# Four seven-product units in each tile from tile 3, with one written order for up projection, attention and down projection

## The chip, the cores and the metric

The kernel runs on one core of a Trainium2 chip. Its time is the device time of one execution in microseconds (us). Seven runs of the kernel before took 279.84 to 280.44 us, with a median of 280.2. The profile is of one further execution.

## The reference: pooled attention, then a two-layer network

The keys and values of 8 batches with 8 heads are averaged over groups of 8 positions (576 rows become 72). Each query attends to the 72 pooled keys of its head. The result, 4608 tokens of 512 values, goes through a network with 2048 hidden values and the silu function.

```python
k_p = k.reshape(B, H, Sp, pool, D).mean(axis=3)      # B = H = 8, S = 576, D = 64, pool = 8, Sp = 72
v_p = v.reshape(B, H, Sp, pool, D).mean(axis=3)
scores = scale * np.matmul(q, k_p.transpose(0, 1, 3, 2))
attn = np.exp(scores - np.max(scores, axis=-1, keepdims=True))
attn = attn / (np.sum(attn, axis=-1, keepdims=True) + 1e-09)
x = np.matmul(attn, v_p).transpose(0, 2, 1, 3).reshape(4608, 512)
h = x @ w_in                                         # 512 x 2048
out = (h / (1 + np.exp(-h))) @ w_out                 # 2048 x 512
```

## The kernel before

**Tiles.** The 4608 tokens are worked off in nine tiles of 512 tokens, tile 0 to tile 8. A tile has an *up half* (`up`), which computes the hidden values `h_T` (16 groups of 128, with tokens as columns) from the attention output `xT`, and a *down half* (`down_quarters`, in tile 0 `down`), which computes the output from them. The attention of batch t+1 is done in between: its parts are small functions (`q_transpose`, `k_transpose`, `scores`, `denominators`, `numerators`), called as *fillers*. Each filler has a step number. `spread` counts the matmul steps of a half, and when a step is reached it issues the fillers due. So the order on every engine is the order in which Python issues instructions; no scheduler changes it, and an engine that waits holds up everything behind it in its own queue.

**Seven products instead of eight.** Some matrix products are split in two by two quarters and computed with seven products of sums of quarters instead of eight products. In the down half that is the whole product (products 1 to 7, each 16 matmuls of 256 columns). It needs five sums of quarters of `w_out` (`weight_sum`, made once), five sums of hidden quarters in each tile (`hidden_sum`, product numbers 1, 2, 5, 6, 7), and additions of the seven results on VectorE and ScalarE. In the up half a *unit* of four hidden groups is split in this way: seven products of four matmuls of 256 columns take the place of 16 matmuls of 512 columns. `UNITS` names three units: A is groups 4 to 7, B 8 to 11 and C 12 to 15. They need sums of `w_in` quarters (`unit_weight_sum`, once) and five sums of `xT` quarters in each tile (`unit_x_sum`). Groups 0 to 3 are *plain*: four matmuls of 512 columns each, followed by a silu. Tile 0 is wholly plain; tile 1 uses units A and B only, and the later tiles all three.

**How a unit goes.** `stage(y, n)` issues product n of unit y and what follows it. Product 2 goes to PSUM bank P and ScalarE copies it to `r_sb`; product 5 goes to bank Q and VectorE adds it to `r_sb`, giving `rr_sb`; product 1 goes to bank R and VectorE subtracts, giving `t_sb`. Products 4 and 3 add onto P and Q, and a silu on ScalarE takes each straight from the bank. Products 7 and 6 add onto P and Q again, and VectorE adds `t_sb`, giving `c_sb[0]` and `c_sb[1]`, from which the stages "h" and "s" make the last two silus. Products 7 and 6 have to wait until the silus of 4 and 3 have read their banks. Each of `r_sb`, `rr_sb`, `t_sb` and the two `c_sb` exists once and is passed from unit to unit. Eight PSUM banks are shared: five in turn for P, Q and the attention (`at`), and three in turn for R, plain groups and the down half (`mm`).

**The down half before.** Order of products: 2, 5, 1, 4, 3, 7, 6. Product 2 is copied to `r_sb` and product 5 is added, giving `rr_sb`; product 1 less `rr_sb` gives `t_sb`. Product 4 onto 2 and product 3 onto 5 are two output quarters (a copy on ScalarE and one on VectorE); 7 and 6 onto these, with `t_sb` added, are the other two. The last tile does products 1, 4, 3, 7, 6 for its first 128 tokens of each half and then for the rest, so that stores can start earlier.

**Other queues.** GpSimd pools keys and values (`pool_k`, `pool_v`) and issues nearly all loads. `behind_x_sums` copies one element of an x sum on GpSimd, so that the pooling starts only when that sum is there. SyncE issues the stores.

Of the kernel before, what the change touches and what calls it, by code (L numbers as in the profile page):

```python
# [27 lines left out]
FP32 = mybir.dt.float32  # L28
# [8 lines left out]
def kernel(  # L37
# [53 lines left out]
    def ps_tile(shape, dtype, tag, name):  # L91
        return psum.tile(shape, dtype, tag=tag, bufs=banks[tag], name=name)
# [24 lines left out]
            singles.tile([128, 5, 2, 256], BF16, name=f"w_sum1{n}") for n in range(2)  # L117
        )
    ]
    x_sum = singles.tile([128, 5, 2, NQ], BF16, name="x_sum")  # L120
    gate = singles.tile([128, 1], BF16, name="gate")
    c_sb = [singles.tile([128, 2, NQ], FP32, name=f"c_sb{n}") for n in range(2)]
# [69 lines left out]
        )  # L192
        nc.gpsimd.tensor_add(out=dst, in0=raw[:, :, :D], in1=raw[:, :, D : 2 * D])

    def behind_x_sums():
        nc.gpsimd.tensor_copy(out=gate[:1], in_=x_sum[:1, U_XI[6], 0, :1])

    def pool_k(b):
        pool_rows(kp[:SP], batches[b]["k_raw"])
# [119 lines left out]
    def third(n):  # L319
        return tuple((g, n * QV, (n + 1) * QV) for g in range(2))  # L320
# [78 lines left out]
    def attn_tables():  # L399
        nc.scalar.preload_act_table_set("natural_log_exp_and_others")  # L400
# [13 lines left out]

    UNITS = ((4, 6), (8, 10), (12, 14))
    UW = [
        {
            (i, j): w_in_sb[:, 2 * j : 2 * j + 2, 128 * u : 128 * (u + 2)]  # L420
# [39 lines left out]
    def up(t, fillers, items):  # L460
# [3 lines left out]
                KF if len(it) == 3 else 2 * len(it[1].strip("hs")) for it in items  # L464
            ),
        )
        ps = {}

        def product(y, n, bank, first):
# [45 lines left out]
            else:  # L515
                hidden(y, 1, 1, c_sb[1])

        for it in items:
            if len(it) == 3:
                plain(t, step, *it)  # L520
            else:
                for n in it[1]:
                    stage(it[0], n)
        for _ in step:
            pass

    def plain(t, step, g, n0, n):
        tag = "at" if (t, g, n0) == (0, 3, 0) else "mm"
# [157 lines left out]
            pass  # L686


    warm_ps = ps_tile([128, 512], FP32, "mm", "warm_ps")

    def warm_up(n):
# [97 lines left out]
        " C6 Ch Cs g2 g3",  # L789
    )  # L790
    visits = [third(n) for n in range(3)]
    for t in range(NT):
        a = t + 1
        f_up, f_down = [], []
        if t == 0:
            GA = 11
# [7 lines left out]
        else:  # L804
            G = lambda *gs: [(g, 0, NTT) for g in gs]
            if t == 1:
                items = (
                    G(12, 13, 14, 15) + [(0, "25143"), (1, "2"), (0, "7"), (1, "5")]
                    + [(0, "6h"), (1, "1"), (0, "s")] + G(0) + [(1, "43")] + G(1)
                    + [(1, "7h6")] + G(2) + [(1, "s")] + G(3)  # L810
                )
            else:
                items = []
                for it in THREE[t // B].split():
                    items += [(("BCA".index(it[0])), it[1])] if it[0] in "ABC" else G(int(it[1]))
# [6 lines left out]
            f_up.append((56, lambda: hidden_sum(6, 4, 8)))  # L822
            for n, k0 in ((2, 0), (5, 0), (1, 4), (1, 0)):
                f_up.append((64, lambda n=n, k0=k0: hidden_sum(n, k0, k0 + 4)))
            f_down.append((33, lambda: hidden_sum(7, 0, 8)))
            f_down.append((71 if t < B else 50, lambda: hidden_sum(6, 0, 4)))

        for n, t0, f_to, at, parts in (
            (1, 0, f_down, 48, (0, PW)), (3, 0, f_down, 52, (0, PW)),
            (6, 0, f_down, 8, (0, PW)), (4, 0, f_down, 12, (0, 2)),  # L830
            (7, 0, f_down, 14, (0, 2)), (4, 1, f_down, 20, (2, PW)), (7, 1, f_down, 52, (2, PW)),
        ):
            for i in range(*parts):
                if t == t0:
                    f_to.append((at + i, lambda n=n, i=i: weight_sum(n, i)))
# [63 lines left out]
        if t == 1:  # L899
            def unit_weight_tiles():  # L900
                k_w = big.tile([128, 4, 2, 256], BF16, tag="k_raw2", name="w_sum12")
                v_w = big.tile([128, 4, 2, 256], BF16, tag="v_raw2", name="w_sum12")
                w_sum1.append([k_w[:, i] for i in range(4)] + [v_w[:, 0]])

            f_down.append((72, unit_weight_tiles))
            for i, n in enumerate(U_W):
                f_down.append((73 if i < 2 else 81, lambda n=n: unit_weight_sum(2, n)))
        if t != 1:
            moe_tables()
        if t == 0:  # L910
# [34 lines left out]
```

## Time and profile before

| | |
|---|---|
| profiled execution | 279.88 us, of which 278.1 us are the span from the first to the last instruction |
| median of seven runs | 280.2 us |
| busy: TensorE, VectorE, ScalarE, GpSimd | 271.7, 220.7, 189.2, 98.3 us |
| a tile with attention (tile 3's down half and tile 4's up half) | 28.77 us |
| silus of plain groups / of units from a bank / from `c_sb` | 592 / 603 and 598 / 628 ns each |
| VectorE addition out of PSUM, 128x512 | 681 to 692 ns each |
| hidden sum, 128x1024 | 684 ns each |
| table load on ScalarE | 1283 ns each |

Busy times are summed over the instructions of an engine. The recorded end of a matmul is modelled, and matmuls are pipelined, so how fast they go is read from the distance of their starts. The order in time shows merged groups: start, length to the last end, engine, line, operation, what it writes and reads, the shape and the count; square brackets give idle time ahead of the group and what ended it. PEld are the weight loads of TensorE.

### The profile page before, as it was taken

The numbers are of one execution on the slowest core, as the hardware profiler recorded it, in microseconds if no ns is written. First come the engines' busy times: TensorE is split into PE (matmuls) and PEld (weight loads), VectorE is DVE, ScalarE is ACT, GpSimd is POOL, SyncE is SP. The second block draws the span as 40 slices with busy tenths as digits, with TensorE's granted clock in tenths as the row PEclk, the third lists the DMA queues.
The fourth block names the chain that finished last, engine by engine and source line by source line (L and its number), as shares of the span: only waits on it lengthen the run. The fifth ranks groups of instructions, "written<-read, shape, count | busy, mean of one in ns | idle before, by whom it ended". The sixth has DMA issues, their size and how long they took to land.

```text
span 278.1 us, 7140 instructions
## 1 busy us (share of the span) xinstructions
PE 271.7 (98%) x2857; PEld 203.2 (73%) x2877; DVE 220.7 (79%) x415; ACT 189.2 (68%) x369; POOL 98.3 (35%) x104
## 2 busy tenths in 40 slices
PE   8999999999999999999999999999999999999995
PEld 4448444576778677867888788687877778788784
DVE  4986777898998976897689768986888588966982
ACT  1688767468577966797679757985789478326810
POOL 8745217142158430953086207970640000000001
PEclk9999999999999999999999999999999999999999
DMA  7999999885849789569756935599510041005004
GB/s 212 279 250 249 205 320 189 236 173 109 160 61 234 202 119 168 134 175 125 148 117 171 132 61 133 143 128 140 133 50 2 2 104 50 0 11 139 7 0 152
DMA packets 31313, 37.71 MB, mean 136 GB/s; under 512 B 10352, under 2 KB 22256, under 8 KB 31280
## 3 DMA queue, kind: packets, MB, share of 16 engines
q0 software_dynamic: 23920, 27.03, 52.0%
q1 hardware_dynamic: 6928, 9.58, 12.5%
q10 hardware_dynamic: 432, 0.66, 0.7%
q8 instruction: 22, 0.36, 0.5%
q14 instruction: 11, 0.09, 0.1%
HBM read 36.70 MB, written 9.44 MB: 166 GB/s over the span
## 4 chain that ended last, share of the span: by engine, by line
PE 79%; DMA 14%; DVE 3%; issue 1%; ACT 1%; POOL 0%; POOLq 0%; DVEq 0%
PE o_psQ L645 16%; PE o_psP L645 16%; PE u_psP L477 11%; PE u_psQ L477 10%; PE hp_ps L537 10%; DMA w_in_sb<-in_moe_w_in_dram 6%; DMA w_out_sb<-in_moe_w_out_dram 6%; PE o_psR L645 5%; PE u_psR L477 3%; PE sc_ps L340 3%; PE nu_ps L384 2%; DMA q_bf<-in_q_dram 2%; PE den_ps L358 2%; DVE w_sum L623 1%; DVE xT L393 1%
## 5 line engine op out<-in xcount | busy, mean ns | idle before, releaser
L645 PEld LDWEIGHTS <-h_sum 128*128 128x128 bf16 x640 | 60.7, 98 | 11.5 <-DVE h_sum L605 1.3
L477 PEld LDWEIGHTS <-w_sum 128*128 128x128 bf16 x460 | 45.0, 98 | 8.4 <-issue 0.5
L605 DVE TENSOR_TENSOR h_sum<-h_T 128x1024 bf16<-128x1024 bf16 (+1 forms) x72 | 49.7, 743 | 1.0 <-ACT h_T L543 1.0
L537 PE MATMUL hp_ps<-xT,w_in_sb 128*128 128x512 bf16 (+3 forms) x253 | 47.8, 329 | 0.8
L348 ACT ACTIVATE es<-sc_ps 72x384 bf16<-72x384 f32 (+1 forms) x100 | 39.0, 469 | 8.5 <-PE sc_ps L340 8.3
L543 ACT ACTIVATE h_T<-hp_ps 128x512 bf16<-128x512 f32 (+2 forms) x63 | 31.7, 520 | 9.9 <-PE hp_ps L537 7.9
L537 PEld LDWEIGHTS <-w_in_sb 128*128 128x128 bf16 x268 | 25.6, 98 | 15.3 <-issue 1.1
L485 ACT ACTIVATE h_T<-c_sb 128x512 bf16<-128x512 f32 x46 | 28.8, 628 | 4.4 <-DVE c_sb L509 3.1
L393 DVE TENSOR_TENSOR xT<-nu_ps,rec 128x384 bf16<-128x384 f32 (+1 forms) x50 | 24.0, 533 | 4.4 <-PE nu_ps L384 4.3
L645 PEld LDWEIGHTS <-h_T 128*128 128x128 bf16 x256 | 24.1, 98 | 4.5 <-issue 0.9
L549 POOL DMA_DIRECT2D out_dram<-o_sb x2 | 1.2, 617 | 67.9 <-issue 67.2
L367 ACT ACTIVATE lnd<-den_ps 128x384 f32<-128x384 f32 (+1 forms) x23 | 11.1, 483 | 19.8 <-PE den_ps L358 19.8
L190 POOL TENSOR_TENSOR raw<-raw 72x1024 f32<-72x1024 f32 x10 | 23.6, 2362 | 0.1
L500 DVE TENSOR_TENSOR t_sb<-u_psR,rr_sb 128x512 f32<-128x512 f32 x23 | 15.9, 692 | 6.7 <-PE u_psR L477 5.0
L494 ACT COPY r_sb<-u_psP 128x512 f32<-128x512 f32 x23 | 13.4, 585 | 10.7 <-PE u_psP L477 8.0
L477 PEld LDWEIGHTS <-w_in_sb 128*128 128x128 bf16 x184 | 17.6, 98 | 2.4
L497 DVE TENSOR_TENSOR rr_sb<-u_psQ,r_sb 128x512 f32<-128x512 f32 x23 | 15.7, 681 | 3.5 <-ACT r_sb L494 1.6
L645 PE MATMUL o_psP<-w_out_sb,h_sum 128*128 128x256 bf16 x128 | 17.6, 273 | 0.0
L512 DVE TENSOR_TENSOR c_sb<-u_psQ,t_sb 128x512 f32<-128x512 f32 x23 | 15.8, 687 | 2.3 <-PE u_psQ L477 2.1
L509 DVE TENSOR_TENSOR c_sb<-u_psP,t_sb 128x512 f32<-128x512 f32 x23 | 15.8, 686 | 2.2 <-PE u_psP L477 0.9
L645 PE MATMUL o_psQ<-w_sum,h_sum 128*128 128x256 bf16 x128 | 16.7, 273 | 0.0
L645 PE MATMUL o_psQ<-w_out_sb,h_sum 128*128 128x256 bf16 x128 | 16.6, 273 | 0.0
(83 smaller groups left out, 508.2 us busy)
## 6 DMA issues: line engine op xcount, KB each, us to landing
out_dram<-o_sb SPq DMA_DIRECT2D x128, 64.0 KB, 1.8
raw<-in_k_dram POOLq DMA_DIRECT2D x10, 576.0 KB, 8.0
raw<-in_v_dram POOLq DMA_DIRECT2D x10, 576.0 KB, 8.0
q_bf<-in_q_dram POOLq DMA_DIRECT2D x6, 576.0 KB, 10.8
w_in_sb<-in_moe_w_in_dram POOLq DMA_DIRECT2D x8, 256.0 KB, 8.5
w_out_sb<-in_moe_w_out_dram POOLq DMA_DIRECT2D x4, 512.0 KB, 13.3
raw<-in_v_dram POOLq DMA_DIRECT2D x2, 768.0 KB, 11.0
raw<-in_k_dram POOLq DMA_DIRECT2D x1, 768.0 KB, 10.4
```

Source lines behind the costliest of these rows:

```text
L190: nc.gpsimd.tensor_add(out=raw[:, :, : 2 * D], in0=raw[:, :, : 2 * D], in1=raw[:, :, 2 * D :])
L348: nc.scalar.activation(es[:, s, :], sc[s], func=AF.Exp, scale=score_scale)
L393: nc.vector.tensor_mul(out=xT[:, 2 * g0 + c : 2 * (g0 + ng - 1) + c + 1 : 2, cols], in0=nu[c][:, :w].rearrange("r (g n) -> r g n", g=ng), ...
L477: nc.tensor.matmul(ps[y, bank][:, u, :], lhsT=w[:, kk, 128 * u : 128 * (u + 1)], rhs=x[:, kk, :], start=first and u == 0 and kk == 0, stop ...
L485: nc.scalar.activation(h_T[:, g : g + 2, j * NQ : (j + 1) * NQ], src, func=AF.Silu)
L500: tt(out=t_sb, in0=ps[y, "R"], in1=rr_sb, op=ALU.subtract)
L509: tt(out=c_sb[0], in0=ps[y, "P"], in1=t_sb, op=ALU.add)
L512: tt(out=c_sb[1], in0=ps[y, "Q"], in1=t_sb, op=ALU.add)
L537: nc.tensor.matmul(hp_ps[:, r0:r1], lhsT=w_in_sb[:, kk, g * 128 : (g + 1) * 128], rhs=xT[:, kk, x0 : x0 + r1 - r0], start=(kk == 0), stop= ...
L543: nc.scalar.activation(h_T[:, g, n0 : n0 + n], hp_ps[:, :n], func=AF.Silu)
L605: nc.vector.tensor_tensor(out=h_sum[n][:, ks, :], in0=quarter(*a, ks), in1=quarter(*b, ks), op=op)
L645: nc.tensor.matmul(ps[b][:, c, :], lhsT=left(n, kt, c), rhs=W_OUT[n][:, kt, :], start=b not in begun, stop=kt == k1 - 1, skip_group_check= ...
```

## The change

From tile 3 on, `up` and `down_quarters` with their fillers are replaced by `run`, which walks through one written order, `PROGRAM`. A token such as `C2` is stage 2 of unit C, and `Ca` and `Cs` are its last two silus; E is a fourth unit, groups 0 to 3, in place of the plain groups. `d40` is the first quarter (four matmuls) of down product 4. `h2h` and `h2l` are the upper and lower half of hidden sum 2. `q`, `k`, `sc`, `de`, `nu` are the parts of attention (`npp` is the last third of the numerators of the batch before), `x4` an x sum, `T1` and `T2` the table loads. Tiles without attention leave these tokens out.

The order of down products becomes 4, 3, 2, 5, 1, 7, 6. Product 4 is copied to `r_sb`, product 3 added to it, and two more VectorE subtractions (`u1`, `u2`) take the two finished output quarters from `rr_sb`; product 1 then adds `rr_sb`. The output quarter of bank Q is copied by ScalarE instead of VectorE. In the last tile products 1, 7, 6 go by columns.

The weight sums of the fourth unit are made in tile 2's down half. In tile 0 the first halves of weight sums 1 and 3 are made at earlier steps. In tile 1 the stage "s" of unit A moves behind stage 4 of unit B, and hidden sum 7 moves from step 33 to 44.

```diff
+    w_e = singles.tile([128, 2, 2, 256], BF16, name="w_sum1e")
...
-    def behind_x_sums():
-        nc.gpsimd.tensor_copy(out=gate[:1], in_=x_sum[:1, U_XI[6], 0, :1])
+    def behind_x_sums(n=6):
+        nc.gpsimd.tensor_copy(out=gate[:1], in_=x_sum[:1, U_XI[n], 0, :1])
...
-    UNITS = ((4, 6), (8, 10), (12, 14))
+    UNITS = ((4, 6), (8, 10), (12, 14), (0, 2))
...
+        stage = unit_stages(t, step)
...
+    def unit_stages(t, step):
         ps = {}
...
+        return stage
...
+    def down_stages(t, last):
+        ps = {}
+        bank = {2: "P", 5: "Q", 1: "R", 4: "P", 3: "Q", 7: "P", 6: "Q"}
+        begun = set()
+        add, sub = ALU.add, ALU.subtract
+        tt = nc.vector.tensor_tensor
+
+        def matmuls(n, k0, k1, cs=(0, 1)):
+            b = bank[n]
+            for kt in range(k0, k1):
+                for c in cs:
+                    nc.tensor.matmul(
+                        ps[b][:, c, :], lhsT=left(n, kt, c), rhs=W_OUT[n][:, kt, :],
+                        start=b not in begun,
+                        stop=kt == k1 - 1, skip_group_check=True,
+                    )
+                    begun.add(b)
+
+        def after(n, cc=(0, 1), tail=False):
+            cs = slice(cc[0], cc[-1] + 1)
+            if n == 4:
+                nc.scalar.copy(r_sb, ps["P"])
+            elif n == 3:
+                tt(out=rr_sb, in0=ps["Q"], in1=r_sb, op=add)
+            elif n == 2:
+                nc.scalar.copy(o_sb[1][:, :, LO], ps["P"])
+                if last:
+                    store(t, 3, LO, (nc.gpsimd,))
+            elif n == 5:
+                nc.scalar.copy(out=o_sb[0][:, :, HI], in_=ps["Q"])
+                if last:
+                    store(t, 1, HI)
+            elif n == 1:
+                tt(out=t_sb[:, cs], in0=ps["R"][:, cs], in1=rr_sb[:, cs], op=add)
+            elif n == 7:
+                tt(out=o_sb[0][:, cs, LO], in0=ps["P"][:, cs], in1=t_sb[:, cs], op=add)
+                for c in cc:
+                    store(t, c, LO if tail else FULL, (nc.scalar if tail else nc.sync,))
+            else:
+                tt(out=o_sb[1][:, cs, HI], in0=ps["Q"][:, cs], in1=t_sb[:, cs], op=add)
+                for c in cc:
+                    if tail:
+                        store(t, 3, HI, both)
+                    else:
+                        store(t, 2 + c, FULL, (nc.gpsimd if last else nc.sync,))
+
+        def part_of(tok):
+            if tok == "o":
+                return after(6)
+            n = int(tok[1])
+            if tok[0] == "u":
+                src = o_sb[1][:, :, LO] if n == 1 else o_sb[0][:, :, HI]
+                nc.vector.tensor_tensor(out=rr_sb, in0=rr_sb, in1=src, op=sub)
+                return
+            if not ps:
+                for b in "PQR":
+                    ps[b] = ps_tile([128, 2, CQ], FP32, "mm", f"o_ps{b}")
+            i = int(tok[2])
+            k0 = 2 * i if n == 4 else 2 * (i ^ 2)
+            matmuls(n, k0, k0 + 2)
+            if i == 3 and n != 6:
+                after(n)
+
+        def columns(c):
+            for n in (1, 7, 6):
+                matmuls(n, 0, KQ, (c,))
+                after(n, (c,), c == 1)
+
+        return part_of, columns
+
+    PROGRAM = (
+        "C2 C5 B2 q0 C1 C4 B5 C3 A2 q1 B4 C7 Ca C6 B1 B3 A5 B7 Cs E2 B6 A1 Ba A3 E5 Bs "
+        "A4 q2 E4 k q3 A6 E3 A7 Aa As E1 h7h E7 E6 d40 npp Ea d41 Es h2h d42 d43 h5h T1 "
+        "h2l d30 d31 d32 d33 sc0 h1l d20 d21 h6l d22 h5l d23 sc1 de0 h1h d50 d51 d52 "
+        "h6h d53 d10 d11 h7l u1 sc2 de1 d12 u2 d13 d70 nu0 d71 de2 nu1 T2 d72 d73 d60 "
+        "x4 x3 d61 x6 d62 x1 d63 o x7 "
+    )
+
+    def run(t):
+        a = t + 1
+        attn, last = a < B, t == NT - 1
+        stage = unit_stages(t, iter(int, 1))
+        part_of, columns = down_stages(t, last)
+        toks = PROGRAM.split()
+        gate_on = int([x for x in toks if x[0] == "x"][-1][1])
+        attn_toks = ("T1 T2 k npp q0 q1 q2 q3 sc0 sc1 sc2 de0 de1 de2 nu0 nu1").split()
+        if last:
+            i = toks.index("d10")
+            sums = [x for x in toks[i:] if x[0] in "hu"]
+            toks = toks[:i] + sums + ["L0", "L1"]
+        toks = [x for x in toks if attn or x not in attn_toks]
+        if a == B - 1:
+            toks.insert(1 + max(toks.index("de2"), toks.index("nu1"), toks.index("o")), "nu2")
+        if t == T4:
+            toks.insert(0, "T2")
+        if attn:
+            if a + 1 < B - 1:
+                load_q(a + 1)
+            behind_x_sums(6 if t == T4 else gate_on)
+            pool_k(a)
+            if a + 1 < B:
+                load_one(a + 1, "k")
+            pool_v(a)
+            if a + 1 < B:
+                load_one(a + 1, "v")
+                if a + 1 == B - 1:
+                    load_q(a + 1)
+                load_rest(a + 1, "k")
+                load_rest(a + 1, "v")
+        for x in toks:
+            if x[0] in "ABCE" and x[1] in "2514376as":
+                stage("ABCE".index(x[0]), {"a": "h"}.get(x[1], x[1]))
+            elif x[0] == "L":
...
+            elif x[:2] == "nu":
+                numerators(a, visits[int(x[2])])
+            elif not last:
+                unit_x_sum(t + 1, int(x[1]))
...
+    T4 = 3
     for t in range(NT):
         a = t + 1
+        if t >= T4:
+            run(t)
+            continue
...
             if t == 1:
                 items = (
                     G(12, 13, 14, 15) + [(0, "25143"), (1, "2"), (0, "7"), (1, "5")]
-                    + [(0, "6h"), (1, "1"), (0, "s")] + G(0) + [(1, "43")] + G(1)
+                    + [(0, "6h"), (1, "1")] + G(0) + [(1, "4"), (0, "s"), (1, "3")] + G(1)
                     + [(1, "7h6")] + G(2) + [(1, "s")] + G(3)
                 )
...
-            f_down.append((33, lambda: hidden_sum(7, 0, 8)))
+            f_down.append((33 if t > 1 else 44, lambda: hidden_sum(7, 0, 8)))
             f_down.append((71 if t < B else 50, lambda: hidden_sum(6, 0, 4)))
...
         for n, t0, f_to, at, parts in (
-            (1, 0, f_down, 48, (0, PW)), (3, 0, f_down, 52, (0, PW)),
+            (1, 0, f_down, 16, (0, 2)), (3, 0, f_down, 30, (0, 2)),
+            (1, 0, f_down, 46, (2, PW)), (3, 0, f_down, 50, (2, PW)),
             (6, 0, f_down, 8, (0, PW)), (4, 0, f_down, 12, (0, 2)),
             (7, 0, f_down, 14, (0, 2)), (4, 1, f_down, 20, (2, PW)), (7, 1, f_down, 52, (2, PW)),
         ):
...
                 k_w = big.tile([128, 4, 2, 256], BF16, tag="k_raw2", name="w_sum12")
                 v_w = big.tile([128, 4, 2, 256], BF16, tag="v_raw2", name="w_sum12")
                 w_sum1.append([k_w[:, i] for i in range(4)] + [v_w[:, 0]])
+                w_sum1.append([v_w[:, 1 + i] for i in range(3)] + [w_e[:, i] for i in range(2)])
 
             f_down.append((72, unit_weight_tiles))
             for i, n in enumerate(U_W):
                 f_down.append((73 if i < 2 else 81, lambda n=n: unit_weight_sum(2, n)))
+        if t == 2:
+            for i, n in enumerate(U_W):
+                f_down.append((76 + 2 * i, lambda n=n: unit_weight_sum(3, n)))
         if t != 1:
             moe_tables()
         if t == 0:
```

## The prediction, made before the changed kernel was run

> **What bounds the kernel now.** I read the first part of the page, then the busy time by stage, then the order in time of single engines.
>
> ```profile
> ## 1 busy us (share of the span) xinstructions
> PE 271.7 (98%) x2857; PEld 203.2 (73%) x2877; DVE 220.7 (79%) x415; ACT 189.2 (68%) x369; POOL 98.3 (35%) x104
> ```
>
> ```profile
> core 0: us, PE busy (x) PEld busy (x) DVE busy (x) ACT busy (x) POOL busy (x), PEclk, DMA share, GB/s
> 237.72:249.97 12.25, 12.25 (x113) 10.82 (x112) 9.53 (x17) 3.33 (x5) 0.00 (x0) 1.00 0.00 1
> 249.97:262.60 12.63, 12.53 (x101) 9.79 (x101) 9.35 (x15) 9.32 (x18) 0.00 (x0) 1.00 0.33 84
> 124.65:153.42 28.77, 28.77 (x342) 24.21 (x340) 23.33 (x42) 22.12 (x43) 12.65 (x10) 1.00 0.71 140
> ```
>
> TensorE sets the time. The first stage is the down half of tile 7 without attention, 112 matmuls of 256 columns; the second the up half of tile 8, 84 of 256 and 16 of 512; the third a whole tile with attention. From 252.15 to 259.13 sixteen unit products start, so one (four matmuls) takes 0.436 us, 109 ns a matmul, at full clock. 28.77 less 12.25 and 12.63 leaves 3.89 us for attention. TensorE stands still nowhere in such a tile, so only its own work, or a wait newly made, can move the time.
>
> Attention is dearer than its matmuls, as this part of TensorE's order in time shows (start, length with a modelled end, what):
>
> ```profile
> 186.83 0.82 PE L645 MATMUL o_psP<-w_sum,h_T 128*128 128x256 bf16 x6
> 187.58 0.35 PE L358 MATMUL den_ps<-es,ones 72*32 72x384 bf16 x4
> 187.75 0.83 PE L384 MATMUL nu_ps<-es,vp 72*32 72x192 bf16 x32
> 188.51 0.94 PE L645 MATMUL o_psP<-w_sum,h_T 128*128 128x256 bf16 x7
> ...
> 223.01 0.61 PE L645 MATMUL o_psQ<-w_sum,h_sum 128*128 128x256 bf16 x4
> 223.55 0.52 PE L384 MATMUL nu_ps<-es,vp 72*32 72x192 bf16 x16
> 224.00 1.26 PE L645 MATMUL o_psQ<-w_sum,h_sum 128*128 128x256 bf16 x10
> ```
>
> Six matmuls of 109 ns from 186.83 end at 187.48; the next full-array matmul starts at 188.51: denominators with two numerators cost 1.03 us. Four from 223.01 end at 223.45, the next is at 224.00: one numerator alone costs 0.55. Read likewise: scores alone 0.56 (151.32 to 151.88), denominators with scores 0.85 (126.39 to 127.24), denominators with one numerator 0.70 (222.31 to 223.01), key transpose 0.13. So a second numerator in a block costs 1.03 - 0.70 = 0.33, alone 0.55: entering and leaving full-array work costs about 0.11 each.
>
> VectorE is the next engine; its order in time:
>
> ```profile
> 146.48 0.68 DVE L509 TENSOR_TENSOR c_sb<-u_psP,t_sb 128x512 f32<-128x512 f32 x1
> 147.08 0.68 DVE L512 TENSOR_TENSOR c_sb<-u_psQ,t_sb 128x512 f32<-128x512 f32 x1
> ...
> 261.75 4.29 DVE L605 TENSOR_TENSOR h_sum<-h_T 128x1024 bf16<-128x1024 bf16 x7
> ```
>
> An instruction lasts 0.68 us but the next starts 0.60 later; seven hidden sums take 4.29, (4.29 - 0.68)/6 = 0.60 apiece. VectorE's room is judged with 0.60.
>
> Tile 1 does have a stall, in TensorE's and ScalarE's order:
>
> ```profile
> 60.82 1.03 PE L537 MATMUL hp_ps<-xT,w_in_sb 128*128 128x512 bf16 x4
> 62.06 0.60 PE L477 MATMUL u_psP<-x_sum,w_sum 128*128 128x256 bf16 x4 [0.21 <-ACT h_T L485]
> ```
>
> ```profile
> 60.40 0.63 ACT L485 ACTIVATE h_T<-c_sb 128x512 bf16<-128x512 f32 x1 [0.57 <-DVE c_sb L512]
> 60.94 0.58 ACT L543 ACTIVATE h_T<-hp_ps 128x512 bf16<-128x512 f32 x1
> 61.42 0.59 ACT L485 ACTIVATE h_T<-u_psP 128x512 bf16<-128x512 f32 x1
> ```
>
> Four matmuls of 217 ns end at 61.69, yet the second unit's product 7 starts at 62.06, when the silu that reads its bank (61.42 to 62.01) is done; the first unit's last silu stands ahead.
>
> **What the Trainium skill says.** "Perfetto Trace Analysis", Identifying the Most-Contended Engine: matmul busy share does not tell how near the roofline a kernel is. The trace agrees (matmuls recorded at 273 ns follow each other at 109), so I count spacing. "TensorE: Matmul & The Clock Gate", Back-to-back issue gap: 262 cycles at 256 columns, 518 at 512, or 109 and 216 ns at 2.4 GHz; the trace has 109 and 217. Its Part 3 says a weight load overlaps running matmuls only where the row groups differ; the 0.11 us at each change of tiling fits that, though the trace does not show the cause. "VectorE: DVE Perf Modes", The TRN2 errata: an fp32 add of 512 takes 691 ns; the trace has 692.
>
> **The change, part by part.**
>
> *Tile 0's weight sums.* Four of the eight sums that run 46.36 to 49.04 (0.335 apart) move to where VectorE idles (0.74 us before 38.82, 1.03 before 43.18). The attention products behind them then follow their numerators (ready about 49.3) and end near 50.4, not 50.99; tile 1's first matmuls no longer wait. 50.60 to 54.27 is 3.67 us for 16 matmuls of 217 ns, 3.47: gain 0.20.
>
> *Tile 1's order.* Without the silu ahead, group 0's runs at 60.15 (matmuls end 59.95, plus 0.20), unit 1's product 4's from 60.65 to 61.25: product 7 starts on time, saving 0.37. The moved silu now stands before product 3's, which ends near 62.28; product 6, due 62.12, waits to 62.32, where it was 62.55. Net 0.20. The hidden sum moved from step 33 to 44 lets value copies start near 71.2, not 72.38: the block at 72.79 takes 0.84 where its like takes 0.70, gain 0.14. Sum of tiles 0 and 1: 0.54.
>
> *Fourth unit's weight sums.* Five VectorE sums, 5 x 0.335 = 1.7 us, in tile 2's down half, where before the stores of products 3 and 7 VectorE idles 1.05 and 1.11 us. Nothing, with that cover; without it at most 0.6.
>
> *Four units from tile 3.* Sixteen plain matmuls become seven products: the up half takes 28 x 0.436 = 12.21 instead of 12.63. Gain 0.42 in each of six tiles.
>
> *Attention in the new order* (tiles 3 to 6). The blocks were scores; denominators+scores; denominators+two numerators; scores; denominators+numerator; transpose: 0.56+0.85+1.03+0.56+0.70+0.13 = 3.83. They become numerator; scores; scores+denominators, twice; numerator; denominators+numerator; transpose: 0.55+0.56+0.85+0.85+0.55+0.70+0.13 = 4.19. Loss 0.36 a tile, three changes of tiling. Denominators *after* scores are not in the trace; bounds 0.70 (denominators add as little as before a numerator) and 0.95 (one more change); I take 0.85, the mirrored order. Net per tile 0.42 - 0.36 = 0.06, times four 0.24.
>
> *VectorE and ScalarE.* Per tile VectorE gains four unit operations and two output differences and loses a copy, 5 x 0.60 = 3.0 us, on 23.3 of 28.8. ScalarE exchanges four silus for a copy, four silus and the output copy, about 1.1 on 22.1. Does either come late? Count from a tile's first product. The unit additions lag about 1.4 us at first (last output sum and x sum) but catch up: product 7 of the first unit ends at 4.36, its addition by 5.3, and the first reuse of its bank, product 5 of the third unit, is due at 5.67. Before the output products VectorE has a chain with no gap: product 7 of the third unit ends at 25 x 0.436 = 10.90, its addition starts 0.26 later, then eleven more up to the low hidden sum of product 5: it starts at 11.16 + 11 x 0.602 = 17.78 and ends at 18.47. With attention, transpose and two products of xT (0.94) make that 19.54, and its reader is due at 42 x 0.436 + 0.13 + 0.55 + 0.56 + 0.85 = 20.40: 0.86 spare. The low sum of product 2 ends at 17.13, its reader is due at 17.81. In tiles 7 and 8 no attention delays TensorE: the reader is due at 18.31, but the sum is there at 18.47, and signal and weight load add about 0.17. Loss 0.33, net 0.42 - 0.33 = 0.09 a tile, two tiles 0.18.
>
> *DMA and GpSimd.* Same instructions in the same order; stores wait for one engine more. GpSimd's gate now follows the last x sum, about 1.4 us into the tile instead of 1.2; pooled keys come near 5.3, wanted at 9.6. In the last column tile two outputs are stored earlier; the last chain of sum and store is unchanged. Zero.
>
> Sum: 0.54 + 0.24 + 0.18 = 0.96 gain. The profiled execution took 279.88 (278.1 of span, 1.8 around it), so 278.9; the runs' median, 280.2, is 0.3 above it, so 279.2.
>
> **Rivals.**
> (a) *The switches are hidden or cheaper*: if denominators cost 0.70 behind scores, 0.30 more returns in each of four tiles, and if the late sum costs nothing in tiles 7 and 8, 0.66 more: gain 2.8, 277.4. For it: weights are loaded ahead. Against: two lone numerators (49 and 223 us) cost 0.55 both.
> (b) *The switches take all*: scores+denominators at 0.95 adds 0.2 a tile, 0.8 in all: 280.0. For it: three array layouts meet in one block.
> (c) *VectorE becomes the bound, slower*: the chain reaches the low sum of product 2 late. It decides where the chain runs 0.5 us late (0.68 less signal and load); 1.1 us late costs 0.6 in each of four tiles, and about 0.6 more in each of the last two: 3.6 lost less 0.96 gained, 282.8; with half that loss, 281.0. It needs a spacing of 0.66 instead of 0.60 over the eighteen or so instructions of a chain. For it: VectorE's load reaches 26.3 of 28.7. Against: 0.60 holds beside busy GpSimd (146 us).
>
> **How the numbers follow.** Forecast 0.50 (its own range 278.7 to 279.7), (a) 0.19, (b) 0.15, (c) 0.16. A difference under 0.2%, 0.56 us, is not told from none: faster is (a) and nearly all of the forecast, 0.67; same is (b) and a remainder, 0.17; slower (c), 0.16. The range 277.4 to 280.6 takes in (a), (b) and the forecast, and leaves out (c).
>
> **What would show it.** Tile 4's period near 28.7, with up products gapless; two lone numerators at 0.55; scores+denominators at 0.85; in tiles 7 and 8 one wait of 0.3 of weight loads on the low hidden sum of product 5; product 7 of tile 1's second unit without its wait. Waits of unit products on VectorE's additions, tile after tile, would make it wrong; so would attention blocks 0.1 off.

## The result, and the profile after

The changed kernel takes 281.4 us (median of 12 runs, 281.15 to 281.65), the kernel before 280.15 (31 runs): ratio 1.0042, 95% interval 1.0034 to 1.0050. That is 1.25 us slower where 1.0 us faster was predicted, so 2.2 us have to be found. The profiled execution took 281.4 us, 279.5 of them span.

The page of the changed kernel, busy time of each engine:

```profile
## 1 busy us (share of the span) xinstructions
PE 273.0 (98%) x2923; PEld 208.8 (75%) x2933; DVE 240.2 (86%) x455; ACT 193.8 (69%) x379; POOL 98.5 (35%) x104
```

TensorE is busy for as large a share as before, while VectorE has gone from 220.7 to 240.2 us. Busy time by stage, the same three stages as before the change (a whole tile with attention, the down half of tile 7, the up half of tile 8):

```profile
core 0: us, PE busy (x) PEld busy (x) DVE busy (x) ACT busy (x) POOL busy (x), PEclk, DMA share, GB/s
...
150.92:179.82 28.90, 28.82 (x338) 23.68 (x336) 26.23 (x48) 23.04 (x45) 13.12 (x11) 1.00 0.60 119
...
238.19:250.82 12.63, 12.40 (x114) 10.87 (x112) 11.79 (x21) 3.71 (x7) 0.00 (x0) 1.00 0.00 1
250.82:263.42 12.60, 12.39 (x115) 10.95 (x113) 10.24 (x18) 8.95 (x17) 0.00 (x0) 1.00 0.33 85
```

No stage became faster by what it saves. The attention tile takes 28.90 us instead of 28.77 (predicted 28.71), the up half of tile 8 12.60 instead of 12.63 (predicted 12.21), the down half of tile 7 12.63 instead of 12.25 (predicted 12.58). In all three the busy time of TensorE is now 0.08 to 0.23 us short of the stage, where before only the second stage fell short (by 0.10). What it waits for is seen in its order in time (start, length, engine, line, operation, matrix multiplied into what bank, shape, count; in brackets the idle time and what ended it):

```profile
176.84 0.29 PE L212 MATMUL kT_ps<-shifts,kp 128*128 128x72 bf16 x4
176.97 0.60 PE L489 MATMUL u_psQ<-x_sum,w_sum 128*128 128x256 bf16 x4
177.65 0.60 PE L489 MATMUL u_psQ<-x_sum,w_in_sb 128*128 128x256 bf16 x4
...
235.20 0.60 PE L489 MATMUL u_psQ<-x_sum,w_sum 128*128 128x256 bf16 x4
236.01 0.60 PE L489 MATMUL u_psQ<-x_sum,w_in_sb 128*128 128x256 bf16 x4 [0.21 <-DVE rr_sb L509]
```

Behind the key transpose (tiles 7 and 8 have none) come two products, each into a bank Q: product 6 of unit A (at 176.97 and 235.20), the third unit in the order of time, and product 3 of unit E, the fourth (at 177.65 and 236.01), which adds onto E's own product 5. Gapless, the second would start 0.44 us after the first. It starts 0.68 later in tile 5 and 0.81 later in tile 7 (the same in tile 8, at 261.24). So 0.24 us are lost in each of tiles 3 to 6 and 0.37 in tiles 7 and 8: 4 x 0.24 + 2 x 0.37 = 1.70 us. What it waits for is `rr_sb` of unit E, since VectorE must have read bank Q before product 3 may add onto it. VectorE's order in time shows why that is late:

```profile
174.69 0.68 DVE L521 TENSOR_TENSOR c_sb<-u_psP,t_sb 128x512 f32<-128x512 f32 x1
175.29 0.68 DVE L524 TENSOR_TENSOR c_sb<-u_psQ,t_sb 128x512 f32<-128x512 f32 x1
176.07 0.69 DVE L512 TENSOR_TENSOR t_sb<-u_psR,rr_sb 128x512 f32<-128x512 f32 x1
176.90 0.69 DVE L509 TENSOR_TENSOR rr_sb<-u_psQ,r_sb 128x512 f32<-128x512 f32 x1
```

From the first to the second of these is 0.60 us, but from the second to the third 0.78 and on to the fourth 0.83. The third writes `t_sb`, which the second reads; the fourth writes `rr_sb`, which the third reads. Each starts 0.10 to 0.14 us after the recorded end of the one before, where an instruction that has nothing to wait for starts 0.08 to 0.09 before it. The fourth ends at 177.59, and product 3 goes on at 177.65.

(Line 489 issues every unit product, line 705 every down product from tile 3 on, line 610 every hidden sum. In kernels with added lines the numbers are a few higher.)

The rest of the loss lies in the down halves without attention:

```profile
243.43 1.04 PE L705 MATMUL o_psQ<-w_out_sb,h_sum 128*128 128x256 bf16 x8
244.70 1.05 PE L705 MATMUL o_psQ<-w_out_sb,h_sum 128*128 128x256 bf16 x8 [0.23 <-DVE h_sum L610]
...
269.93 1.05 PE L705 MATMUL o_psQ<-w_out_sb,h_sum 128*128 128x256 bf16 x8 [0.23 <-DVE h_sum L610]
...
272.62 1.04 PE L705 MATMUL o_psQ<-w_sum,h_sum 128*128 128x256 bf16 x8
273.66 1.03 PE L705 MATMUL o_psR<-w_sum,h_sum 128*128 128x256 bf16 x8
```

The second half of product 5 starts 1.27 us after the first instead of 0.87: 0.40 in each of tiles 7 and 8. In tile 8 product 1 of the second column starts at 273.66, 0.17 after its turn (272.62 + 0.87): it shares bank R with the first column, which VectorE must have read.

Tiles 0 and 1 show what the prediction said of product 7 of the second unit, in TensorE's and ScalarE's order:

```profile
61.73 0.60 PE L489 MATMUL u_psP<-x_sum,w_sum 128*128 128x256 bf16 x4
62.33 0.60 PE L489 MATMUL u_psQ<-x_sum,w_sum 128*128 128x256 bf16 x4
```

```profile
60.68 0.59 ACT L497 ACTIVATE h_T<-u_psP 128x512 bf16<-128x512 f32 x1
61.16 0.63 ACT L497 ACTIVATE h_T<-c_sb 128x512 bf16<-128x512 f32 x1
61.68 0.60 ACT L497 ACTIVATE h_T<-u_psQ 128x512 bf16<-128x512 f32 x1
```

Product 7 starts when the matmuls ahead end (60.86 + 4 x 0.217 = 61.73), and product 6, due at 62.17, starts at 62.33, behind the silu that ends at 62.28.

### The profile page after: what moved, and what is told of

Read it like the earlier page. It is cut to its first block, busy times and chain, and to the rows that moved or that the text cites. A ratio compares the mean times of both kernels' runs of the same rounds, so it can differ in the third digit from the quotient of the medians.

```text
span 279.5 us, 7356 instructions
## 1 busy us (share of the span) xinstructions
PE 273.0 (98%) x2923; PEld 208.8 (75%) x2933; DVE 240.2 (86%) x455; ACT 193.8 (69%) x379; POOL 98.5 (35%) x104
## 4 chain that ended last, share of the span: by engine, by line
PE 74%; DMA 14%; DVE 9%; issue 2%; POOL 0%; DVEq 0%; POOLq 0%
PE u_psP L489 12%; PE u_psQ L489 11%; PE o_psQ L705 10%; PE o_psP L705 9%; DMA w_in_sb<-in_moe_w_in_dram 6%; DMA w_out_sb<-in_moe_w_out_dram 6%; PE u_psR L489 5%; PE o_psR L705 4%; PE o_psQ L650 4%; PE o_psP L650 4%; PE hp_ps L542 4%; PE sc_ps L341 3%; PE nu_ps L385 3%; PE o_ps L577 2%; DMA q_bf<-in_q_dram 2%; DVE h_sum L610 2%
## 5 line engine op out<-in xcount | busy, mean ns | idle before, releaser
L489 PEld LDWEIGHTS <-w_sum 128*128 128x128 bf16 x532 | 51.7, 98 | 7.1 <-issue 0.3
L705 PEld LDWEIGHTS <-h_sum 128*128 128x128 bf16 x480 | 45.1, 98 | 9.5 <-issue 2.2
L497 ACT ACTIVATE h_T<-c_sb 128x512 bf16<-128x512 f32 x58 | 35.6, 626 | 13.3 <-DVE c_sb L521 13.1
L542 PE MATMUL hp_ps<-xT,w_in_sb 128*128 128x512 bf16 (+2 forms) x151 | 25.9, 317 | 0.3
L489 PEld LDWEIGHTS <-w_in_sb 128*128 128x128 bf16 x232 | 22.5, 98 | 4.6 <-issue 1.8
L548 ACT ACTIVATE h_T<-hp_ps 128x512 bf16<-128x512 f32 (+2 forms) x39 | 18.1, 477 | 5.8 <-PE hp_ps L542 4.8
L542 PEld LDWEIGHTS <-w_in_sb 128*128 128x128 bf16 x156 | 14.6, 98 | 8.5 <-issue 0.8
L705 PEld LDWEIGHTS <-h_T 128*128 128x128 bf16 x192 | 18.5, 98 | 2.7 <-issue 0.6
L489 PE MATMUL u_psQ<-x_sum,w_in_sb 128*128 128x256 bf16 x116 | 17.5, 272 | 0.7 <-DVE rr_sb L509 0.4
L497 ACT ACTIVATE h_T<-u_psQ 128x512 bf16<-128x512 f32 x29 | 17.1, 590 | 1.0 <-PE u_psQ L489 0.7
L497 ACT ACTIVATE h_T<-u_psP 128x512 bf16<-128x512 f32 x29 | 16.7, 598 | 1.2 <-PE u_psP L489 1.1
```

The source lines that it names most:

```text
L489: nc.tensor.matmul(ps[y, bank][:, u, :], lhsT=w[:, kk, 128 * u : 128 * (u + 1)], rhs=x[:, kk, :], start=first and u == 0 and kk == 0, stop ...
L497: nc.scalar.activation(h_T[:, g : g + 2, j * NQ : (j + 1) * NQ], src, func=AF.Silu)
L542: nc.tensor.matmul(hp_ps[:, r0:r1], lhsT=w_in_sb[:, kk, g * 128 : (g + 1) * 128], rhs=xT[:, kk, x0 : x0 + r1 - r0], start=(kk == 0), stop= ...
L705: nc.tensor.matmul(ps[b][:, c, :], lhsT=left(n, kt, c), rhs=W_OUT[n][:, kt, :], start=b not in begun, stop=kt == k1 - 1, skip_group_check= ...
```

## The experiments

My theory: the loss is the wait of the fourth unit's product 3, and that wait comes from the single `rr_sb` and `t_sb`, which make VectorE's neighbours wait for each other. Rivals: VectorE simply has too much to do, whatever the buffers; the order of the products is at fault; the attention blocks cost more than predicted; the tile 0 and 1 edits lose time. All differences below are of medians, against the kernel before (280.07 to 280.15, run beside each experiment) or against the changed kernel's 281.40, which was not run again beside them.

**Tiles 0 and 1 alone**, on the kernel before:

```diff
-                    + [(0, "6h"), (1, "1"), (0, "s")] + G(0) + [(1, "43")] + G(1)
+                    + [(0, "6h"), (1, "1")] + G(0) + [(1, "4"), (0, "s"), (1, "3")] + G(1)
...
-            f_down.append((33, lambda: hidden_sum(7, 0, 8)))
+            f_down.append((33 if t > 1 else 44, lambda: hidden_sum(7, 0, 8)))
...
-            (1, 0, f_down, 48, (0, PW)), (3, 0, f_down, 52, (0, PW)),
+            (1, 0, f_down, 16, (0, 2)), (3, 0, f_down, 30, (0, 2)),
+            (1, 0, f_down, 46, (2, PW)), (3, 0, f_down, 50, (2, PW)),
```

> The kernel before with the edits of tiles 0 and 1 alone (weight sums sooner, the silu moved, hidden sum 7 later). If these edits work as the trace after suggests (TensorE's start of tile 2's up half 0.17 us earlier although the first matmul of tile 1 came 0.26 later), they are worth 0.43 us: 279.7 us. Rival: what they give is taken back in tile 1's down half, where denominators now wait for a late ScalarE: 280.1 us.

279.68 us, ratio 0.9984 (0.9977 to 0.9991): 0.45 us faster than before. So this part of the change gains what it should within 0.1. Tile 2, where the fourth unit's weight sums are made, takes 28.74 us in the changed kernel and 28.73 here, so the loss is wholly in the new order from tile 3 on: 281.40 - 279.68 = 1.72 us slower than without it, where 0.42 faster was predicted.

**Two buffers**: the changed kernel with a second `rr_sb` and `t_sb` for every other unit. They take the place of small early buffers that are no longer used from tile 3 on, and a buffer of reciprocals goes from four to three.

```diff
         def stage(y, n):
+            odd = t >= T4 and y % 2
+            rr, ts = (rr_2, t_2) if odd else (rr_sb, t_sb)
...
-                tt(out=rr_sb, in0=ps[y, "Q"], in1=r_sb, op=ALU.add)
+                tt(out=rr, in0=ps[y, "Q"], in1=r_sb, op=ALU.add)
...
-                tt(out=t_sb, in0=ps[y, "R"], in1=rr_sb, op=ALU.subtract)
+                tt(out=ts, in0=ps[y, "R"], in1=rr, op=ALU.subtract)
```

> The changed kernel with a second rr_sb and t_sb that every other unit uses, everything else in its order (the buffers lie over tiles that are dead after tile 1, and three buffers of reciprocals in place of four). Theory: single buffers make VectorE wait for its own last instruction (0.78 and 0.83 us from start to start in place of 0.60), so the fourth unit's rr comes late and its product 3 waits 0.24 us in each of four tiles and 0.37 in each of the last two, 1.7 us in all: 279.7 us, and the waits are gone. Rival, VectorE simply has too much work: the wait stays or turns up at a later product, 281.2 us.

279.52 us, 1.88 less than the changed kernel and 0.998 (0.9972 to 0.9988) of the one before. VectorE does the same number of instructions (455), but without the pauses. Its order (three lines from one unit earlier, and unit E's `rr_sb`) and TensorE's:

```profile
172.00 0.68 DVE L531 TENSOR_TENSOR c_sb<-u_psQ,t_sb 128x512 f32<-128x512 f32 x1
172.59 0.68 DVE L519 TENSOR_TENSOR t<-u_psR,rr 128x512 f32<-128x512 f32 x1
173.19 0.68 DVE L516 TENSOR_TENSOR rr_sb<-u_psQ,r_sb 128x512 f32<-128x512 f32 x1
...
175.77 0.69 DVE L516 TENSOR_TENSOR rr<-u_psQ,r_sb 128x512 f32<-128x512 f32 x1
```

```profile
176.50 0.60 PE L494 MATMUL u_psQ<-x_sum,w_sum 128*128 128x256 bf16 x4
176.94 0.60 PE L494 MATMUL u_psQ<-x_sum,w_in_sb 128*128 128x256 bf16 x4
```

The distances are 0.59 and 0.60. Unit E's `rr_sb` ends at 176.46, 0.48 before product 3, which follows product 6 after 0.44. The wait of product 5 in tiles 7 and 8 falls from 0.40 to 0.21 as well. With the same amount of work on VectorE, "too much to do" is out for this wait.

**The second `rr_sb` only**: as above, but both units' `t_sb` stay one buffer.

```diff
-            rr, ts = (rr_2, t_2) if odd else (rr_sb, t_sb)
+            rr, ts = (rr_2, t_sb) if odd else (rr_sb, t_sb)
```

> The changed kernel with a second rr_sb only; t_sb stays single. The distance from t_sb to rr_sb should fall from 0.83 to about 0.60, that from c_sb to t_sb stay at 0.78. The fourth unit's rr_sb then comes 0.2 to 0.25 sooner, which is nearly the whole wait of product 3 in tiles 3 to 6 (0.24) and some two thirds of it in tiles 7 and 8 (0.37): the time falls by 4 x 0.22 + 2 x 0.23 = 1.3, to about 280.1. If the single t_sb is what holds VectorE up, it falls by less than 0.4, to 281.0 or more.

279.99 us, 1.41 less than the changed kernel. VectorE's order:

```profile
174.68 0.68 DVE L531 TENSOR_TENSOR c_sb<-u_psQ,t_sb 128x512 f32<-128x512 f32 x1
175.47 0.69 DVE L519 TENSOR_TENSOR t_sb<-u_psR,rr_sb 128x512 f32<-128x512 f32 x1
176.07 0.68 DVE L516 TENSOR_TENSOR rr<-u_psQ,r_sb 128x512 f32<-128x512 f32 x1
```

The pause ahead of the single `t_sb` stays (0.79), the one ahead of the doubled `rr_sb` is gone (0.60). So each pause belongs to its own buffer. Product 3 follows after 0.44 in each of the six tiles, so all of its 1.70 us of waiting are gone. The expected gain of 1.3 was met in part by luck: it left a third of the wait in tiles 7 and 8 standing. About 0.3 us is lost again at the end, where 4.4 us pass from the start of the last product to the end of the span instead of 4.1. The other kernels with two buffers made from the changed one show 4.3 to 4.4 there; why stays open. What the second `t_sb` adds, 0.47, is mostly the sooner hidden sums of tiles 7 and 8: here product 5 still waits 0.39 in tile 7 (242.22 to 243.48 is 1.26 instead of 0.87).

**Two buffers in the kernel before**, the control:

> The kernel before with a second rr_sb and t_sb from tile 3 on, given to every other unit. VectorE's distances of 0.79 to 0.83 between unit operations are in its trace too, but plain groups lie between the units there and no TensorE wait is seen. If what costs is the wait of the fourth unit's product 3, and not the distances as such, the kernel before gains nothing: 280.15 (279.9 to 280.4). If the distances cost time by themselves (the rival: any relief of VectorE helps), it gains about as the changed kernel did, 1 to 1.9: 278.3 to 279.2.

The edit is that of the two buffers, with its side effects (early buffers overlaid, three buffers of reciprocals). 280.22 us, ratio 1.0006 (0.9997 to 1.0014): nothing, so the side effects are no gain by themselves. Its tile takes 28.77 us as before (first unit product of tile 4 at 138.63, of tile 5 at 167.40), though VectorE's distance from `t_sb` to `rr_sb` fell there from 0.83 to 0.61. A pause costs time only where TensorE is waiting at its end; in the kernel before, where plain groups lie between the units, it was not.

**Product 3 later**: the changed kernel with E's product 3 behind A's product 7.

```diff
-        "A4 q2 E4 k q3 A6 E3 A7 Aa As E1 h7h E7 E6 d40 npp Ea d41 Es h2h d42 d43 h5h T1 "
+        "A4 q2 E4 k q3 A6 A7 E3 Aa As E1 h7h E7 E6 d40 npp Ea d41 Es h2h d42 d43 h5h T1 "
```

> The changed kernel with the fourth unit's product 3 behind the third unit's product 7 instead of ahead of it, 0.44 us later in TensorE's order. Theory (one wait at one place): product 3 finds its bank free, 1.7 us back, 279.7 us. Rival (VectorE's rate is the bound): the wait moves to the next reader of VectorE's results and the time stays at 281.2.

280.52 us, 0.88 less than the changed kernel. The profiled execution took 281.62, 1.1 above this median, but it lost that ahead of tile 1, whose first matmul starts at 51.96 instead of 50.86, so the later tiles can be read. TensorE and ScalarE:

```profile
177.92 0.60 PE L489 MATMUL u_psQ<-x_sum,w_sum 128*128 128x256 bf16 x4
178.54 0.60 PE L489 MATMUL u_psP<-x_sum,w_sum 128*128 128x256 bf16 x4
178.97 0.60 PE L489 MATMUL u_psQ<-x_sum,w_in_sb 128*128 128x256 bf16 x4
```

```profile
177.38 0.62 ACT L497 ACTIVATE h_T<-c_sb 128x512 bf16<-128x512 f32 x1
177.90 1.07 ACT L497 ACTIVATE h_T<-u_psP 128x512 bf16<-128x512 f32 x2
```

Product 3 (third line) now waits for nothing, but product 7 ahead of it starts at 178.54 instead of 178.36. It adds onto bank P, which the first of the two silus at 177.90 reads. That silu stands in a row without a gap on ScalarE, which begins at 175.82 with a copy into `r_sb`, and VectorE, late by its pauses, reads `r_sb` until 175.73 (read from the times; not tested). The wait moved: it is 0.18 in each of tiles 3 to 6 and 0.3 in tiles 7 and 8, 1.3 in all, so only 0.4 of the 1.70 came back here. The other 0.4 is product 5 in tiles 7 and 8, which waits 0.21 instead of 0.40. This order alone doesn't cure it.

**The low hidden sum of product 5 sooner**, in tiles 7 and 8 of the changed kernel:

```diff
+        if not attn:
+            toks.remove("h5l")
+            toks.insert(1 + toks.index("d33"), "h5l")
```

> The changed kernel with the low hidden sum of product 5 ahead of those of 1 and 6 in tiles 7 and 8 only. If the 0.40 us gap in product 5 is this sum's place in VectorE's queue: 0.8 us back, 280.6 us. If VectorE's rate is the bound there, product 1 waits in its place: 281.3 us.

281.06 us: 0.34 of 0.8. In tile 7 the down half falls from 12.63 to 12.36; in tile 8 nothing is gained (11.98 from the first down product to the last group, in both kernels), because another sum is late in its place:

```profile
269.86 1.04 PE L705 MATMUL o_psR<-w_sum,h_sum 128*128 128x256 bf16 x8
271.19 1.05 PE L705 MATMUL o_psP<-w_sum,h_sum 128*128 128x256 bf16 x8 [0.29 <-DVE h_sum L610]
```

**Two buffers, and all hidden sums of tiles 7 and 8 in the order of need:**

```diff
+        if not attn:
+            toks = (
+                " ".join(toks[: toks.index("d33") + 1]).replace(" h1l", "").replace(" h6l", "")
+                + " h5l h1h d20 d21 h1l d22 d23 h7l d50 d51 h6h d52 d53 h6l "
+                + ("u1 u2 L0 L1" if last else
+                   "d10 d11 u1 d12 u2 d13 d70 d71 d72 d73 d60 x4 x3 d61 x6 d62 x1 d63 o x7")
+            ).split()
```

> The kernel with two rr_sb and t_sb, and in tiles 7 and 8 (without attention) the hidden sums of the down half in the order in which TensorE needs them. With two buffers alone the time was 279.5. What that kernel still waits: 0.21 before the second half of product 5 in tiles 7 and 8, 0.1 to 0.2 before product 1 in tile 8. If these are only an order on VectorE, the time falls by 0.4 to 0.7, to 278.9 to 279.1. If VectorE has too much to do in that stretch, the wait moves on to products 1 and 7 and the time stays at 279.3 to 279.6.

279.12 us, ratio 0.9962 (0.9950 to 0.9974), 0.40 less than with two buffers alone. TensorE:

```profile
242.50 1.91 PE L712 MATMUL o_psQ<-w_out_sb,h_sum 128*128 128x256 bf16 x16
244.25 1.91 PE L712 MATMUL o_psR<-w_sum,h_sum 128*128 128x256 bf16 x16
...
270.44 1.04 PE L712 MATMUL o_psQ<-w_sum,h_sum 128*128 128x256 bf16 x8
271.76 1.03 PE L712 MATMUL o_psR<-w_sum,h_sum 128*128 128x256 bf16 x8 [0.27 <-DVE t_sb L734]
```

Product 5 takes its 1.75 us, and tile 7 has no wait left. In tile 8 the wait of product 1's second column for bank R has grown from 0.17 to 0.45 (270.44 + 0.87 = 271.31, start 271.76). What it waits for ends a row on VectorE without a gap:

```profile
269.69 1.48 DVE L753 TENSOR_TENSOR rr_sb<-rr_sb,o_sb 128x512 f32<-128x512 f32 x2
271.28 0.42 DVE L734 TENSOR_TENSOR t_sb<-o_psR,rr_sb 128x256 f32<-128x256 f32 x1
```

These are `u1`, `u2` and the sum behind them. Each reads what the one ahead wrote, and they start about 0.80 apart (an instruction of 0.68 leaves 1.48 - 0.68 = 0.80 for the first two). At 0.60 apart the last would start 0.39 sooner, an estimate from these distances, so most of this wait, too, would be pauses. A second buffer can't remove these, since a value passes from one to the next. That VectorE simply has too much to do is thus not shown in tile 8 either. Another order there was not run.

**What a change of tiling costs.** First on the kernel before: the numerators of the previous batch done by themselves, six steps later, instead of beside others.

```diff
-                    f_down.append((nu_at[n], lambda: numerators(a - 1, visits[2])))
+                    f_down.append((62, lambda: numerators(a - 1, visits[2])))
```

> The kernel before with one edit: the third numerators of the previous batch are done by themselves, at step 62 of the down half instead of 56, where they stood beside other numerators. TensorE then changes once more in each tile from full matmuls to matmuls over parts of the array and back. If the change and the return cost 0.21 us together, as the prediction has it, in each of five tiles, the time rises by about 1.1, from 280.15 to 281.2. If they cost nothing by themselves (the time lies in the blocks, wherever they stand): 280.15.

281.31 us, ratio 1.0036 (1.0024 to 1.0048): 1.16 us slower, 0.23 for each of five tiles. TensorE's order shows the two blocks that were one:

```profile
159.58 0.35 PE L358 MATMUL den_ps<-es,ones 72*32 72x384 bf16 x4
159.76 0.50 PE L384 MATMUL nu_ps<-es,vp 72*32 72x192 bf16 x16
160.19 0.83 PE L645 MATMUL o_psP<-w_sum,h_T 128*128 128x256 bf16 x6
160.95 0.51 PE L384 MATMUL nu_ps<-es,vp 72*32 72x192 bf16 x16
161.40 0.28 PE L645 MATMUL o_psP<-w_sum,h_T 128*128 128x256 bf16 x1
```

Six full matmuls end at 160.85 and the next starts at 161.40: the lone numerators cost 0.55, as the prediction read elsewhere. Nothing else in this kernel is changed, so the price is that of leaving full-array matmuls once more and coming back.

Then on the changed kernel, the opposite: the second denominators and the lone numerators moved beside the first numerators.

```diff
-        "A4 q2 E4 k q3 A6 E3 A7 Aa As E1 h7h E7 E6 d40 npp Ea d41 Es h2h d42 d43 h5h T1 "
+        "A4 q2 E4 k q3 A6 E3 A7 Aa As E1 h7h E7 E6 d40 Ea d41 Es h2h d42 d43 h5h T1 "
...
-        "h6h d53 d10 d11 h7l u1 sc2 de1 d12 u2 d13 d70 nu0 d71 de2 nu1 T2 d72 d73 d60 "
+        "h6h d53 d10 d11 h7l u1 sc2 d12 u2 d13 d70 de1 npp nu0 d71 de2 nu1 T2 d72 d73 d60 "
```

> The changed kernel with one edit in the written order: the second denominators and the third numerators of the batch before are done directly beside the first numerators, so that in tiles 3 to 6 TensorE changes three times less often between matmuls over the whole array and matmuls over parts of it. If each such change costs what the prediction read from the trace (about 0.11 us to go over and as much to come back), the attention of a tile takes 3.8 instead of 4.16 us, and the time falls by some 0.36 x 4 = 1.4, from 281.4 to about 280.0. Rival: what was moved now comes late for its readers (the bank that the third denominators take is free only after a ScalarE instruction that waits for the second), a new wait of 0.1 to 0.3 us per tile takes most of it: 280.5 to 281.4.

TensorE then changes its tiling three times less in a tile: it leaves full-array matmuls once less (over and back), and one block of scores has no denominators behind it. 280.43 us, 0.97 less than the changed kernel where 1.4 was expected: 0.24 a tile. In the trace the down half of tile 4 falls from 16.31 to 16.05. The block of denominators and two numerators costs 1.03, as it did before the change; 0.07 to 0.08 of the rest went into a short wait within the second scores (their 16 matmuls take 0.61 instead of 0.54), which the next kernel doesn't have.

**All three together** (two buffers, order of need, denominators beside numerators):

> The changed kernel with two rr_sb and t_sb, the hidden sums of tiles 7 and 8 in the order of need, and the denominators and numerators of tiles 3 to 6 side by side. If the three are independent: 279.0 less 1.4, about 277.6. If the grouping only moves a wait: 278.5 to 279.0. Both are below the 280.15 of the kernel before.

278.02 us, ratio 0.9919 (0.9906 to 0.9932) to the kernel before: 2.1 us faster than it, 3.4 faster than the changed kernel. Putting the denominators beside the numerators brings 1.1 here (from 279.12; five and six runs) where 1.4 was expected, so the time lies between the two that were expected. The block in TensorE's order:

```profile
160.99 0.60 PE L712 MATMUL o_psP<-w_sum,h_sum 128*128 128x256 bf16 x4
161.52 0.35 PE L364 MATMUL den_ps<-es,ones 72*32 72x384 bf16 x4
161.70 0.83 PE L390 MATMUL nu_ps<-es,vp 72*32 72x192 bf16 x32
162.46 0.61 PE L712 MATMUL o_psP<-w_sum,h_sum 128*128 128x256 bf16 x4
```

A tile with attention (first down product at 150.26 to the next at 178.60) takes 28.34 us. The kernel before took 28.77: the difference, 0.43, is just what the fourth unit saves in matmuls (0.42). With the waits and the extra changes of tiling gone, the saving arrives whole in such a tile. The wait that is left on VectorE is the one in tile 8, 0.44 here.

## Why the prediction was wrong

The step that failed is the one headed "VectorE and ScalarE". It counted VectorE's chain with one distance, 0.60 us, and looked at three readers: the first reuse of a bank (product 5 of the third unit), and the low sums of products 2 and 5. Two things were wrong in it.

*The distance.* 0.60 holds for the seven hidden sums from which it was read, because they do not wait for each other. Unit additions write what their neighbour reads: four of them take 0.60 + 0.78 + 0.83 + 0.60 = 2.81 us instead of 2.40. The evidence stood in the trace before, in the very stretch from which two lines were quoted: there the additions at 145.05 and 145.88 lie 0.83 apart, those at 147.08 and 147.87 0.79. Only the pair that suited the sum was used. The additions of that stretch, in the kernel before:

```profile
145.05 0.69 DVE L500 TENSOR_TENSOR t_sb<-u_psR,rr_sb 128x512 f32<-128x512 f32 x1
145.88 0.69 DVE L497 TENSOR_TENSOR rr_sb<-u_psQ,r_sb 128x512 f32<-128x512 f32 x1
...
147.87 0.69 DVE L500 TENSOR_TENSOR t_sb<-u_psR,rr_sb 128x512 f32<-128x512 f32 x1
```

*The reader.* Product 3 of the fourth unit must wait until VectorE has read bank Q. The additions of units B, A and E stand there in one unbroken row, and this deadline was not checked. A check with 0.60 would have found no wait: with two buffers, where the distances are 0.60, `rr_sb` is done 0.48 before product 3 starts. So the distance is the term that failed, and this reader is where it came out. Measured: 1.70 us of waiting in six tiles. One buffer more, at no work, took all of these waits away and returned 1.41 of the time; both returned 1.88.

The other terms, with what was predicted and what the runs and the trace showed:

| step | predicted | measured |
|---|---|---|
| tiles 0 and 1 | -0.54 | -0.45 (alone, by medians) |
| fourth unit, each of six up halves | -0.42 | -0.43 without its wait (tile 4: 12.79 before; after 12.60, of which 0.24 is wait) |
| attention in the new order, each of four tiles | +0.36 | +0.33 (down half 15.98 to 16.31 us) |
| low sum of product 5, tiles 7 and 8 | +0.33 each | +0.40 each |
| product 1's second column, tile 8 | 0 | +0.17, and 0.07 ahead of products 7 and 6 |
| fourth unit's product 3 | 0 | +1.70 in all |

The last two lines, 0.14 from the line above them and 0.1 from the first make 1.70 + 0.24 + 0.14 + 0.1 = 2.2. Less 4 x 0.03 from the attention and 6 x 0.01 from the fourth unit, that is 2.0 of the 2.2 us; the remaining 0.2 is not accounted for.

In tiles 0 and 1 the parts came out as 0.20 (first matmuls), 0.27 (order of silus; predicted 0.20; from the first matmul of tile 1 to its down half it is 13.63 instead of 14.10, which is both) and 0.14 (the numerators' block at 72.67 takes 0.70), but tile 1's denominators with scores now take 1.03 us instead of 0.84, which takes 0.19 back. They read the exponentials from ScalarE. With the tile 0 and 1 edits alone these end at 68.57, as in the kernel before, while TensorE reaches the denominators at 68.42 instead of 68.86: it came sooner, ScalarE did not.

*Rivals.* (a), cheaper changes of tiling, is refuted twice: 1.16 us were lost by leaving and returning once more in five tiles, and 0.97 regained by three changes less in each of four (0.08 a change, or 0.10 with the short wait counted in). The Trainium skill, "TensorEngine Tiling (Array Packing)", Key Properties, says that changing the tiling mode drains TensorE; it gives no price, and these runs put it at 0.23 us for going over and coming back (0.19 to 0.22 by the two tiles read in the trace, 28.96 and 28.99 us instead of 28.77). Why it costs that stays open. The prediction's remark on weight loads does not explain it: in full-array work, where every load takes all rows, loads of 98 ns go with matmuls 109 ns apart, so they do overlap. (b) fell too: scores with denominators cost 0.84, not 0.95. (c), VectorE as the bound with 281.0 to 282.8, had the engine, the kind of cause (a distance larger than 0.60) and the time right. Its place was wrong: it looked at the low sum of product 2, behind which no wait appears, and it set the distance against the whole chain, where it was two buffers between units. It was given 0.16 because 0.60 "holds beside busy GpSimd"; that was the wrong disturbance to ask about.

The prediction's list of what would make it wrong did name "waits of unit products on VectorE's additions, tile after tile", and that is what came.

## What to carry to other kernels

Where a change packs an engine more densely, don't count its chain with the spacing of independent instructions: look in the trace at each pair in which one writes what its neighbour reads, and, where the neighbour only waits to overwrite, give that buffer a second copy before changing any order. Check the deadline of every instruction that waits for this engine, those included that only wait until a bank has been read. A saving in matmuls can be paid back in changes between full-array and partial matmuls, so keep the small work together.

## What was not expected of the hardware

VectorE's additions of 0.68 to 0.69 us out of PSUM start 0.59 to 0.61 us apart when they are independent, and 0.78 to 0.83 apart when the second writes a buffer that the first still reads; with a second buffer for one of the two, just its own pause went (0.83 to 0.60). The Trainium skill, "VectorE: DVE Perf Modes", The DRAIN you can't avoid, says of eight copies that a semaphore after each of them costs nothing extra. For these additions it is otherwise: waiting for the instruction just ahead costs 0.18 to 0.23 us, and the measurement decides. The write was held up although no value passes through that buffer from the first to the second instruction; where a value does pass, as in the row of `u1` and `u2` above, the distance is about 0.80 as well.
